# One decode step, attention over a cached K and V: ScalarE sums 80 positions of a middle step, TensorE none

## The chip, the cores and the metric

The kernel runs on one core of a Trainium2 chip. The metric is the time of one execution on the device, in microseconds. Three runs of the kernel before took 665.63, 665.69 and 666.15 us; the median is 665.69.

## The reference

A layer of a decoder for two sequences (B = 2) that each add one token. The attention has 32 heads of 128, each with its own cached K and V of 8192 positions; behind it comes a gated feed-forward part with a width of 1376.

```python
def _A_ref(x, k_cache, v_cache, wq, wo):
    q = transpose((x @ wq).reshape(B, Sq, Hq, Dh), 0, 2, 1, 3)      # Sq = 1, Hq = 32, Dh = 128
    scores = einsum("bhqd,bhkd->bhqk", q, k_cache) * (Dh ** -0.5)   # 8192 positions
    p = softmax(scores)
    o = einsum("bhqk,bhkd->bhqd", p, v_cache)
    return transpose(o, 0, 2, 1, 3).reshape(B, Sq, Hq * Dh) @ wo
def _B_ref(x, W_gate, W_up, W_down):
    gate = x @ W_gate
    h = gate * (gate > 0) * (x @ W_up)
    return h @ W_down
h = x + _A_ref(layernorm(x), k_cache, v_cache, wq, wo)
out = h + _B_ref(layernorm(h), W_gate, W_up, W_down)
```

K and V together are 268 of the 281 MB that the program reads, all in bfloat16.

## The kernel before

**Steps.** K and V come in steps of four heads of one sequence (NH = 4). There are 16 such groups. Steps 0 to 14 are quads; the last group is cut into two halves of two heads, steps 15 and 16 (p0 and p1 in the code). Q = LASTQ = 14 is the last quad; a "middle step" is one below it. A quad's K is a tile of 128 partitions by 32768 elements: 32 partitions to a head, and on each partition 256 positions of 128 elements. So one column of the scores is one position per partition, and a step has 256 columns.

**Buffers.** Three buffers of this size hold K and V in turn: K of step i is in buffer 2i mod 3, V in buffer 2i+1 mod 3 (with exceptions at the end). K of a step and V of the next share a buffer, and so do V of a step and K of the one after next. V of step i+1 can be loaded only once the scores of step i are done with its K, and K of step i+2 only once the values matmuls of step i are done with its V. All these loads are issued by SP, in program order, through `load_tile` (L156 to 163).

**Scores, three ways.** The columns of a step are divided among three engines.

- TensorE scores the last `npe` columns (`scores_pe`, L315): it transposes them in groups of eight into PSUM, ScalarE copies them back (L339), TensorE multiplies with q, which `place_q` has put into the zero-padded `qz` (L277), ScalarE copies the rows out (L347), TensorE turns them, ScalarE puts them into the score columns `scol` (L356).
- For all other columns (`nv`) VectorE multiplies K with q in place (`products`, L360, rows L364).
- Of these, ScalarE sums the first `na` columns, one ACTIVATE with an accumulator to a column (`act_sums`, L366, rows L372), and VectorE the rest, by halving four times (L384) and one reduction (L386) (`scores`, L376).

In a middle step `npe` is 24 and `na` 24; step 0 has `npe` 32; steps 14, 15 and 16 have `npe` 16; steps 15 and 16 have `na` 16.

**Softmax and values.** VectorE takes each partition's maximum (`pm`, L390). TensorE spreads it (`largest`, L397), VectorE reduces it to the negative maximum of each head (`nm`, L402), ScalarE takes four exponentials (L407), and TensorE multiplies 64 times with V (`values`, L420). ScalarE copies the result to `pv` (L425).

**Finished heads.** After steps 3, 7, 11 and 14 a group of heads is finished. `close` (L305) sums the denominators (`z_ps`), takes the reciprocal (`rz`, L299) and normalises (L303). It is called in the step after the group's last. In step 12, `spread` (L455) and `lay_rows` (L466, L467) also lay the first 16 heads out as rows for the projection with wo.

**Order.** The schedule is written by hand; each engine works in program order. In a middle step i of the kernel before: scores of TensorE for step i, q of step i+1 placed, the large products of step i, the sums of VectorE, V of step i+1 loaded, the spread of the maximum, `nm` and exponentials, the first 24 columns of the products of step i+1, ScalarE's 24 sums of them, `close` and (in step 12) `lay_rows`, the values of step i, and K of step i+2 loaded. In step 13 the first products of step 14 stand in front of `nm` of step 13; in step 14 the first products of p0 stand in front of its `nm`.

**The end.** Behind step 14 come wo in pieces, V of p0 and p1, the feed-forward weights, the two halves, the projection, the second layer norm and the feed-forward part.

Of the kernel before, what the change touches and what calls it, by code (L numbers as in the profile page):

```python
# [13 lines left out]
def _free(t, offset, dims):  # L14

    return bass.AP(tensor=t.tensor, offset=t.offset + offset, ap=[t.ap[0]] + [list(d) for d in dims])
# [7 lines left out]
def kernel(  # L24
# [14 lines left out]
    P = nc.NUM_PARTITIONS  # L39
# [8 lines left out]
    f32 = mybir.dt.float32  # L48
# [4 lines left out]
    LASTQ = B * NQ - 2  # L53
# [3 lines left out]
    VG = 4  # L57


    NPE = 24  # L60
    NPE_AT = {0: 32, LASTQ: 16, LASTQ + 1: 16, LASTQ + 2: 16}
    NACT = 24
    NACT_AT = {LASTQ + 1: 16, LASTQ + 2: 16}
    QZ = 32


# [15 lines left out]
    small = ctx.enter_context(tc.tile_pool(name="small", bufs=1))  # L82
# [43 lines left out]
    class Step:  # L126
        def __init__(self, i):
# [9 lines left out]
            else:  # L137
# [6 lines left out]
                self.pg, self.zc = pgp[:, k], zc[:, self.b, self.g, 2 * k:2 * k + 2]  # L144
            self.npe = NPE_AT.get(i, NPE)
            self.nv = self.nt - self.npe
            self.na = NACT_AT.get(i, NACT)
            self.hp = P // self.nh
# [4 lines left out]
    steps = [Step(i) for i in range(LASTQ + 3)]  # L153
    Q = LASTQ
# [28 lines left out]
    with tc.manual_schedule():  # L183
# [92 lines left out]
        def place_q(s):  # L276
            nc.scalar.activation(out=qz[:, QZ - NH:QZ], in_=qTs[:, s.b, NH * s.g:NH * (s.g + 1)], func=ACT.Copy)  # L277
# [27 lines left out]
        def close(i):  # L305
# [4 lines left out]
        scols = {  # L310
            i: qrep[:, c0:c0 + n].rearrange("p i d -> p (i d)").bitcast(f32)
            for i, c0, n in ((Q, 6, 4), (Q + 1, 10, 2), (Q + 2, 12, 2))
        }

        def scores_pe(s, between=lambda: None):  # L315


            U = s.npe // 4
            nh, nv = s.nh, s.nv
            row_ps = ps.tile([nh * U, 4 * P], f32, tag="row")  # L320

            def times_q(c0):
                for k in range(0, TPC, 4):
                    u = (c0 + k) // 4
                    if s.quad:
                        z = qz[:, QZ - NH - NH * u:QZ - NH - NH * u + NH * U]
                    else:
                        z = qzp[:, s.k, 14 - 2 * u:14 - 2 * u + 2 * U]
                    nc.tensor.matmul(  # L329
                        out=row_ps, lhsT=z, rhs=s.kt[:, (nv + c0 + k) * Dh:(nv + c0 + k + 4) * Dh],  # L330
                        start=(u == 0), stop=(u == U - 1),
                    )

            for c0 in range(0, s.npe, TPC):
                t_ps = ps2.tile([P, TPC, P], bf16, tag="tp")
                for k in range(TPC):
                    t = nv + c0 + k
                    nc.tensor.transpose(t_ps[:, k, :], s.kt[:, t * Dh:(t + 1) * Dh], ident)  # L338
                nc.scalar.activation(  # L339
                    out=s.kt[:, (nv + c0) * Dh:(nv + c0 + TPC) * Dh], in_=t_ps.rearrange("p t s -> p (t s)"), func=ACT.Copy,  # L340
                )
                between()
                if c0:
                    times_q(c0 - TPC)
            times_q(s.npe - TPC)
            rows = s.kt[0:nh * U, nv * Dh:nv * Dh + 8 * P].bitcast(f32)
            nc.scalar.activation(out=rows, in_=row_ps, func=ACT.Copy)  # L347
            between()
            sc_ps = ps.tile([P, 4, U, nh], f32, tag="row", name="sc_ps")
            for t in range(4):  # L350
                nc.tensor.transpose(  # L351
                    sc_ps[:, t].rearrange("p u j -> p (u j)"), rows[:, t * P:(t + 1) * P], ident_f[0:nh * U, 0:nh * U],
                )
            for j in range(nh):
                r = s.rows(j)
                nc.scalar.activation(  # L356
                    out=scols[s.i][r, nv:s.nt].rearrange("p (u t) -> p t u", t=4), in_=sc_ps[r, :, :, j], func=ACT.Copy,
                )

        def products(s, t0=0, t1=None):  # L360

            n = (s.nv if t1 is None else t1) - t0
            kv = _free(s.kt, t0 * Dh, [[Dh, n], [1, Dh]])
            nc.vector.tensor_tensor(out=kv, in0=kv, in1=_free(s.qr, 0, [[0, n], [1, Dh]]), op=ALU.mult)  # L364

        def act_sums(s, t0=0, t1=None):  # L366

            if t0 == 0 and s.i < Q:
                scols[s.i] = small.tile([P, s.nt], f32, tag="scol", name="scol")
            for t in range(t0, s.na if t1 is None else t1):  # L370
                kv = s.kt[:, t * Dh:(t + 1) * Dh]
                nc.scalar.activation(out=kv, in_=kv, func=ACT.Copy, accum_out=scols[s.i][:, t:t + 1])  # L372
# [3 lines left out]
        def scores(s):  # L376

            scol = scols[s.i]
            width = Dh
            while width > 8:  # L380
                half = width // 2
                lo = _free(s.kt, s.na * Dh, [[Dh, s.nv - s.na], [1, half]])
                hi = _free(s.kt, s.na * Dh + half, [[Dh, s.nv - s.na], [1, half]])
                nc.vector.tensor_tensor(out=lo, in0=lo, in1=hi, op=ALU.add)  # L384
                width = half
            nc.vector.tensor_reduce(  # L386
                out=scol[:, s.na:s.nv], in_=_free(s.kt, s.na * Dh, [[Dh, s.nv - s.na], [1, 8]]), axis=AXIS.X, op=ALU.add,
            )
            pms[s.i] = small.tile([P, 1], f32, tag="pm", name="pm", bufs=2)
            nc.vector.tensor_reduce(out=pms[s.i], in_=scol, axis=AXIS.X, op=ALU.max)  # L390
# [59 lines left out]
        def spread(k, b):  # L450

            h0, n, _ = SETS[k]
            nq = Dh // n
            sp = qrep[:, B * k + b, :]
            nc.vector.tensor_tensor(  # L455
                out=_free(sp, 0, [[nq, n], [1, nq]]), in0=_free(ocol, h0 * B + b, [[B, n], [0, nq]]),
                in1=_free(quot[n], 0, [[0, n], [1, nq]]), op=ALU.mult,
            )
            return sp

        def lay_rows(k, sps):

            r = SROWS[k]
            or_ps = ps.tile([P, B, r], f32, tag="mx")
            for b in range(B):
                nc.tensor.matmul(out=or_ps[:, b, :], lhsT=sps[b], rhs=rest[r], start=True, stop=True)  # L466
            nc.vector.tensor_copy(orow[k], or_ps.rearrange("p b c -> p c b"))  # L467
# [14 lines left out]
                    start=False, stop=(h == Hq - 1), skip_group_check=True,  # L482
                )

        place_q(steps[0])
        for i in range(Q):
            s = steps[i]
            if i == 0:
                products(s, 0, s.na)
                act_sums(s)  # L490
            scores_pe(s)
            place_q(steps[i + 1])
            products(s, s.na)
            scores(s)
            if i == Q - 2:
                load_tile(A_k_cache, steps[Q], steps[Q].kt)
            else:
                load_tile(A_v_cache, steps[i + 1], steps[i + 1].vt)
            if i == Q - 1:
                scores_pe(steps[Q])  # L500
            largest(s)
            if i == Q - 1:
                products(steps[Q], 0, steps[Q].nv // 4)
            exponentials(s)
            if i < Q - 1:
                products(steps[i + 1], 0, steps[i + 1].na)
            act_sums(steps[i + 1])
            if i - 1 in groups:
                close(i - 1)
            if i == 12:  # L510
                lay_rows(0, [spread(0, b) for b in range(B)])
            half = s.nt // VG // 2
            values(s, 0, half)
            if i == Q - 1:
                load_tile(A_k_cache, steps[Q + 1], steps[Q + 1].kt)
            values(s, half, 2 * half)
            if i in groups:
                diagonals(i)
            if i + 2 < Q:
                load_tile(A_k_cache, steps[i + 2], steps[i + 2].kt)  # L520
            elif i == Q - 2:
                load_tile(A_v_cache, steps[Q - 1], steps[Q - 1].vt)
            else:
                load_tile(A_k_cache, steps[Q + 2], steps[Q + 2].kt)


        s, p0, p1 = steps[Q:]
        products(s, s.nv // 4)
        scores(s)
        load_tile(A_v_cache, p0, p0.vt)  # L530
        largest(s)
        products(p0, 0, p0.nv // 4)
        exponentials(s)
        for k, (h0, n, at) in enumerate(SETS):
            nc.sync.dma_start(
# [8 lines left out]
            out=wo[:, (HM + 2) * D:Hq * D].rearrange("p (h n) -> p h n", n=D),  # L544
            in_=_dram(A_wo, (HM + 2) * Dh * D, [[D, P], [Dh * D, 2], [1, D]]),
        )
        products(p0, p0.nv // 4)

        done = [0]
        parts = [0, 6, 8, 10]  # L550

        def values_then_sums():
            some_values()
# [6 lines left out]
                done[0] += 8  # L560

        scores_pe(p0, values_then_sums)
        act_sums(p0, 10)
        some_values()
        load_tile(A_v_cache, p1, p1.vt, pieces=4)
        scores(p0)
# [90 lines left out]
        parts = [(range(0, UP), "of", ps), (range(UP, FC), "tp", ps2)]  # L657
# [53 lines left out]
```

## Time and profile before

| | |
|---|---|
| median of three runs | 665.69 us |
| the profiled execution's own time | 665.04 us |
| its span, first to last instruction | 663.2 us |
| TensorE, matmuls | 359.2 us busy, 54% of the span |
| VectorE | 524.0 us, 79% |
| ScalarE | 243.6 us, 37% |
| GpSimd | 5.1 us, 1% |
| DMA | 281.45 MB, mean 424 GB/s |
| granted TensorE clock, mean | 0.748 |

How to read it: the span is a little shorter than the execution's time. Busy shares are means over the span; a share of DMA engines of 1.00 in a stretch means that all 16 engines moved data all through it, and a stretch can show a little over 1 since a packet's share is not always counted where it falls. PE is TensorE's matmuls, PEld its weight loads, DVE VectorE, ACT ScalarE, SPq the queue of SP that issues the loads. "<-" behind an idle time names what ended it. In the trace of before, `products` is L364, `act_sums` L372, `scores` L384 to L390; in the kernel after, some of these lines move up by one.

### The profile page before, as it was taken

To read this page: it belongs to the slowest core of one execution; us is meant where nothing else is said; L and a number is where in the kernel's file an instruction comes from. 1 tells how busy PE (TensorE), PEld (TensorE's weight loads), DVE (VectorE), ACT (ScalarE), POOL (GpSimd) and SP (SyncE) were. 2 spreads that over 40 slices of the span, in tenths; PEclk is the share of its full clock that TensorE was granted. 3 is DMA by queue.
4 is the path that set the end of the run, shared out by engine and by line. 5 is a ranking of instruction groups with operands and counts; after the bars stand their busy time and mean duration, and the time that the engine had idled before them with its cause. 6 is when DMAs were issued, how large, how long until landed. Compare 5 with 4: busy or idle time off the path is not lost.

```text
span 663.2 us, 5777 instructions
## 1 busy us (share of the span) xinstructions
PE 359.2 (54%) x2103; PEld 164.0 (25%) x2103; DVE 524.0 (79%) x210; ACT 243.6 (37%) x1083; POOL 5.1 (1%) x25
## 2 busy tenths in 40 slices
PE   3530925729184561918358291754819248281996
PEld 1220311304032220403114140321304124130455
DVE  1398696969969596996969699596978959997981
ACT  1171433515153351515335151532614253431650
POOL 2000000000000000000000000000000000000000
PEclk9865775959678695967859596685959659595885
DMA  9999999999999999999999999999999998999997
GB/s 380 443 440 443 443 432 395 443 443 432 435 440 431 415 444 443 419 440 439 435 428 431 443 424 431 431 436 435 435 440 435 423 440 360 423 404 435 422 390 275
DMA packets 8568, 281.45 MB, mean 424 GB/s; under 512 B 858, under 2 KB 2012, under 8 KB 3420
## 3 DMA queue, kind: packets, MB, share of 16 engines
q1 hardware_dynamic: 8536, 281.09, 98.6%
q8 instruction: 16, 0.26, 0.1%
q14 instruction: 12, 0.10, 0.0%
q10 hardware_dynamic: 4, 0.00, 0.0%
HBM read 281.09 MB, written 0.00 MB: 424 GB/s over the span
## 4 chain that ended last, share of the span: by engine, by line
DMA 40%; DVE 39%; PE 17%; ACT 2%; issue 1%; SPq 0%; DVEq 0%; ACTq 0%
DMA tile<-in_A_k_cache_dram 30%; DVE tile L364 19%; DVE tile L384 17%; PE pv_ps L420 15%; DMA tile<-in_A_wo_dram 5%; DMA tile<-in_B_W_up_dram 2%; ACT pgq L407 2%; DVE scol L386 2%; DMA tile<-in_A_wq_dram 2%; PE q_ps L244 1%; DMA tile<-in_B_W_down_dram 1%; PE mx_ps L397 1%; DVE pm L390 0%; DVE nm L402 0%; DVE qrep L386 0%
## 5 line engine op out<-in xcount | busy, mean ns | idle before, releaser
L364 DVE TENSOR_TENSOR tile<-tile,qrep 128x3072 bf16<-128x3072 bf16 (+4 forms) x30 | 235.7, 7887 | 79.8 <-DMA tile<-in_A_k_cache_dram 79.8
L420 PE MATMUL pv_ps<-tile,pgq 128*16 128x512 bf16 x960 | 242.9, 420 | 43.6 <-ACT pgq L407 37.1
L384 DVE TENSOR_TENSOR tile<-tile 128x13312 bf16<-128x13312 bf16 (+7 forms) x68 | 217.7, 3202 | 2.3
L372 ACT ACTIVATE tile<-tile 128x128 bf16<-128x128 bf16 x392 | 114.8, 294 | 72.6 <-DVE tile L364 72.5
L420 PEld LDWEIGHTS <-pgq 128*16 128x16 bf16 x960 | 91.8, 97 | 188.4 <-issue 48.7
L397 PE MATMUL mx_ps<-nscale,pm 128*128 128x128 f32 x34 | 13.2, 491 | 184.9 <-DVE pm L390 184.9
L407 ACT ACTIVATE pgq<-scol,nm 32x256 bf16<-32x256 f32 x56 | 28.3, 505 | 178.6 <-DVE nm L402 177.6
L372 ACT ACTIVATION_READ_ACCUMULATOR tile<-tile 128x1 f32 x392 | 73.0, 186 | 0.0
L397 PEld LDWEIGHTS mx_ps<-nscale,pm 128*128 128x128 f32 x34 | 8.3, 306 | 187.3 <-DVE pm L390 175.8
L339 ACT ACTIVATE tile<-t_ps 128x1024 bf16<-128x1024 bf16 x49 | 48.5, 1021 | 14.3 <-PE t_ps L338 14.0
L329 PE MATMUL row_ps<-tile,qz 128*24 128x512 bf16 (+2 forms) x90 | 28.4, 398 | 26.4 <-ACT tile L339 26.4
L425 ACT ACTIVATE pv<-pv_ps 16x512 f32<-16x512 f32 (+1 forms) x16 | 9.4, 588 | 69.9 <-PE pv_ps L420 69.9
L338 PE MATMUL t_ps<-ident,tile 128*128 128x128 bf16 x392 | 30.1, 231 | 7.8 <-DMA tile<-in_A_k_cache_dram 7.8
L338 PEld LDWEIGHTS <-tile 128*128 128x128 bf16 x392 | 24.2, 104 | 21.6 <-issue 13.3
L386 DVE TENSOR_REDUCE scol<-tile 128x208 f32<-128x1664 bf16 (+1 forms) x14 | 26.3, 1882 | 1.4
L364 DVE TENSOR_TENSOR tile<-tile,qpair 128x7168 bf16<-128x7168 bf16 (+2 forms) x4 | 15.5, 3884 | 4.1 <-DMA tile<-in_A_k_cache_dram 4.1
L402 DVE TENSOR_REDUCE nm<-mx_ps 128x4 f32<-128x128 f32 (+1 forms) x17 | 4.9, 291 | 14.3 <-PE mx_ps L397 14.3
L329 PEld LDWEIGHTS <-qz 128*24 128x24 bf16 (+2 forms) x90 | 7.1, 92 | 35.8 <-issue 31.0
L347 ACT ACTIVATE tile<-row_ps 24x512 f32<-24x512 f32 (+3 forms) x17 | 10.0, 586 | 13.3 <-PE row_ps L329 13.3
L247 DVE CAST tile<-q_ps 2x512 bf16<-2x512 f32 x8 | 5.4, 679 | 11.8 <-PE q_ps L244 11.8
L244 PE MATMUL q_ps<-tile,xn 128*2 128x512 bf16 x32 | 10.0, 477 | 8.6 <-DMA tile<-in_A_wq_dram 8.6
L356 ACT ACTIVATE scol<-sc_ps 32x24 f32<-32x24 f32 (+1 forms) x56 | 11.5, 205 | 8.2 <-PE sc_ps L351 7.2
(117 smaller groups left out, 129.9 us busy)
## 6 DMA issues: line engine op xcount, KB each, us to landing
tile<-in_A_k_cache_dram SPq DMA_DIRECT2D x2, 4096.0 KB, 24.1
tile<-in_A_wq_dram SPq DMA_DIRECT2D x1, 4096.0 KB, 12.3
tile<-in_A_v_cache_dram SPq DMA_DIRECT2D x1, 4096.0 KB, 23.8
tile<-in_A_v_cache_dram SPq DMA_DIRECT2D x4, 1024.0 KB, 12.5
tile<-in_A_wo_dram SPq DMA_DIRECT2D x1, 2048.0 KB, 28.2
tile<-in_B_W_gate_dram SPq DMA_DIRECT2D x1, 1376.0 KB, 16.0
tile<-in_B_W_up_dram SPq DMA_DIRECT2D x2, 688.0 KB
tile<-in_A_wo_dram SPq DMA_DIRECT2D x1, 1024.0 KB, 30.2
```

The lines of the kernel that those rows point to most:

```text
L244: nc.tensor.matmul(out=q_ps, lhsT=xn[:, c, :], rhs=wq_sb[:, c, n0:n0 + 4 * Dh], start=(c == 0), stop=(c == KC - 1),)
L329: nc.tensor.matmul(out=row_ps, lhsT=z, rhs=s.kt[:, (nv + c0 + k) * Dh:(nv + c0 + k + 4) * Dh], start=(u == 0), stop=(u == U - 1),)
L338: nc.tensor.transpose(t_ps[:, k, :], s.kt[:, t * Dh:(t + 1) * Dh], ident)
L339: nc.scalar.activation(out=s.kt[:, (nv + c0) * Dh:(nv + c0 + TPC) * Dh], in_=t_ps.rearrange("p t s -> p (t s)"), func=ACT.Copy,)
L356: nc.scalar.activation(out=scols[s.i][r, nv:s.nt].rearrange("p (u t) -> p t u", t=4), in_=sc_ps[r, :, :, j], func=ACT.Copy,)
L364: nc.vector.tensor_tensor(out=kv, in0=kv, in1=_free(s.qr, 0, [[0, n], [1, Dh]]), op=ALU.mult)
L372: nc.scalar.activation(out=kv, in_=kv, func=ACT.Copy, accum_out=scols[s.i][:, t:t + 1])
L384: nc.vector.tensor_tensor(out=lo, in0=lo, in1=hi, op=ALU.add)
L386: nc.vector.tensor_reduce(out=scol[:, s.na:s.nv], in_=_free(s.kt, s.na * Dh, [[Dh, s.nv - s.na], [1, 8]]), axis=AXIS.X, op=ALU.add,)
L397: nc.tensor.matmul(out=mx[s.i], lhsT=_free(pms[s.i], 0, [[0, P]]), rhs=nscale, start=True, stop=True)
L407: nc.scalar.activation(out=s.pg[r, :, j, :], in_=scol[r, :].rearrange("p (u t) -> p u t", t=VG), func=ACT.Exp, scale=SCALE, bias=nm[r, j:j ...
L420: nc.tensor.matmul(out=pv_ps[s.i][r, :], lhsT=s.pg[:, u].rearrange("p j t -> p (j t)"), rhs=s.vt[:, u * VG * Dh:(u + 1) * VG * Dh], start= ...
```

## The change

- In steps 0 to 13 TensorE scores no columns any more (`npe` 0): `scores_pe` and `place_q` are called for step 14 and the halves alone.
- In these steps ScalarE sums the first 80 columns instead of 24. VectorE multiplies all 256 columns, instead of 232 (224 in step 0), and sums 176 instead of 208 (200 in step 0).
- In step 14 ScalarE sums 64 columns instead of 24 (VectorE 176 instead of 216), in each half 24 instead of 16 (VectorE 88 instead of 96).
- The products that are made ahead for the next step have 48 columns instead of 24, and ScalarE sums these 48 ahead; the remaining 32 follow once the large products of the step are issued.
- The products ahead and their sums are put behind `close` and `lay_rows` in program order. In steps 13 and 14, `nm` no longer has the first products of the next step in front of it.
- The score columns are allocated by `column` instead of in `act_sums`.

```diff
-    NPE = 24
-    NPE_AT = {0: 32, LASTQ: 16, LASTQ + 1: 16, LASTQ + 2: 16}
-    NACT = 24
-    NACT_AT = {LASTQ + 1: 16, LASTQ + 2: 16}
+    NPE = 0
+    NPE_AT = {LASTQ: 16, LASTQ + 1: 16, LASTQ + 2: 16}
+    NACT = 80
+    NACT_AT = {LASTQ: 64, LASTQ + 1: 24, LASTQ + 2: 24}
+    NEXT = 48
...
-            if t0 == 0 and s.i < Q:
-                scols[s.i] = small.tile([P, s.nt], f32, tag="scol", name="scol")
...
-        place_q(steps[0])
+        def column(s):
+            scols[s.i] = small.tile([P, s.nt], f32, tag="scol", name="scol")
+
+        column(steps[0])
+        products(steps[0], 0, NEXT)
+        act_sums(steps[0], 0, NEXT)
         for i in range(Q):
             s = steps[i]
-            if i == 0:
-                products(s, 0, s.na)
-                act_sums(s)
-            scores_pe(s)
-            place_q(steps[i + 1])
-            products(s, s.na)
+            products(s, NEXT)
+            act_sums(s, NEXT)
             scores(s)
             if i == Q - 2:
                 load_tile(A_k_cache, steps[Q], steps[Q].kt)
             else:
                 load_tile(A_v_cache, steps[i + 1], steps[i + 1].vt)
-            if i == Q - 1:
-                scores_pe(steps[Q])
             largest(s)
-            if i == Q - 1:
-                products(steps[Q], 0, steps[Q].nv // 4)
             exponentials(s)
-            if i < Q - 1:
-                products(steps[i + 1], 0, steps[i + 1].na)
-            act_sums(steps[i + 1])
             if i - 1 in groups:
                 close(i - 1)
             if i == 12:
                 lay_rows(0, [spread(0, b) for b in range(B)])
+            if i + 1 < Q:
+                column(steps[i + 1])
+            products(steps[i + 1], 0, NEXT)
+            act_sums(steps[i + 1], 0, NEXT)
             half = s.nt // VG // 2
             values(s, 0, half)
...
+        place_q(steps[Q])
+        scores_pe(steps[Q])
         s, p0, p1 = steps[Q:]
-        products(s, s.nv // 4)
+        products(s, NEXT)
+        act_sums(s, NEXT)
         scores(s)
         load_tile(A_v_cache, p0, p0.vt)
         largest(s)
-        products(p0, 0, p0.nv // 4)
         exponentials(s)
...
-        products(p0, p0.nv // 4)
+        products(p0, 0, p0.na)
+        products(p0, p0.na)
...
-        parts = [0, 6, 8, 10]
+        parts = [0, 8, 16, 20]
...
-        act_sums(p0, 10)
+        act_sums(p0, 20)
```

## The prediction

> **What bounds the kernel now.** I read the page's slices first, then the busy shares by stretch, then the order of the work inside one middle step, and last the place where the DMA share falls. The slices:
>
> ```profile
> DMA  9999999999999999999999999999999998999997
> GB/s 380 443 440 443 443 432 395 443 443 432 435 440 431 415 444 443 419 440 439 435 428 431 443 424 431 431 436 435 435 440 435 423 440 360 423 404 435 422 390 275
> ```
>
> The DMA engines are busy nearly everywhere, while VectorE (DVE) has 79% of the span and ScalarE (ACT) 37%. The busy shares by stretch say it sharper (columns: stretch, its length, busy time of PE, PEld, DVE, ACT, POOL, then the granted clock, the DMA share and GB/s):
>
> ```profile
> 304.80:382.68 77.88, 43.26 (x212) 19.20 (x211) 63.85 (x18) 29.33 (x132) 0.00 (x0) 0.76 1.00 433
> ...
> 460.58:538.44 77.86, 39.64 (x205) 17.98 (x202) 63.84 (x18) 29.33 (x132) 0.00 (x0) 0.76 1.01 435
> ...
> 550.00:562.00 12.00, 10.02 (x63) 4.54 (x62) 11.97 (x2) 4.10 (x5) 0.00 (x0) 1.00 0.79 317
> 562.00:592.00 30.00, 17.57 (x85) 7.68 (x85) 29.66 (x10) 13.81 (x68) 0.00 (x0) 0.72 0.98 422
> ```
>
> The first two are two middle steps each: share 1.00, so 38.9 us per step is the time to bring in 16.8 MB, and nothing that engines do faster shortens it. One stretch, 550 to 562, has share 0.79: the engines ran dry. The timeline around it shows why (start, duration, engine, line, operation, idle time before it):
>
> ```profile
> 538.44 1.76 DVE L364 TENSOR_TENSOR tile<-tile,qrep 128x3072 bf16<-128x3072 bf16 x1 [5.43 <-DMA tile<-in_A_k_cache_dram]
> 540.12 0.25 DVE L299 RECIPROCAL rz<-z_ps 128x16 f32<-128x16 f32 x1
> ...
> 540.50 0.48 DVE L455 TENSOR_TENSOR qrep<-ocol,quot 128x128 bf16<-128x128 bf16 x2
> 540.84 0.39 PE L466 MATMUL or_ps<-rest,qrep 128*128 128x16 bf16 x2 [7.16 <-DVE qrep L455]
> 541.16 15.45 PE L420 MATMUL pv_ps<-tile,pgq 128*16 128x512 bf16 x64
> ...
> 556.64 0.33 SPq L161 DMA_DIRECT2D tile<-in_A_v_cache_dram  x1
> ```
>
> This is step 12. Its exponentials ended at 535.57, but TensorE first has to lay the finished heads (L466), which waits for VectorE, which stands at the products of step 13 until K of step 13 lands at 538.44. So the values matmuls start at 541.16, end at 556.6, and only then can SP load V of step 13 into their buffer. The transfer ahead (K of step 14, issued at 531.45) had drained by about 554. Everywhere else the next load is issued about 7 us before the one ahead lands, for instance in step 7:
>
> ```profile
> 306.65 0.31 ACT L372 ACTIVATE tile<-tile 128x128 bf16<-128x128 bf16 x1 [5.31 <-DVE tile L364]
> 306.86 0.19 ACT L372 ACTIVATION_READ_ACCUMULATOR tile<-tile 128x1 f32 x1
> 306.96 0.29 ACT L372 ACTIVATE tile<-tile 128x128 bf16<-128x128 bf16 x1
> ...
> 336.36 0.42 DVE L390 TENSOR_REDUCE pm<-scol 128x1 f32<-128x256 f32 x1
> 336.40 0.33 SPq L161 DMA_DIRECT2D tile<-in_A_v_cache_dram  x1
> ...
> 343.40 1.76 DVE L364 TENSOR_TENSOR tile<-tile,qrep 128x3072 bf16<-128x3072 bf16 x1 [5.45 <-DMA tile<-in_A_k_cache_dram]
> ```
>
> V is issued at 336.40, K ahead of it lands at 343.40. Call the landing of a step's K (here 304.80) L: scores end at L+31.6, the next K lands at L+38.6 to 38.9.
>
> **The change, part by part.**
>
> *Middle step, VectorE.* Products grow by 24 positions, sums shrink from 208 to 176. Slopes come from rows of two sizes: products 26624 elements in 14.018 us and 3072 in 1.758, so 0.521 ns each: +1.60 us. The four additions fall from 7.09+3.62+1.89+1.02 = 13.63 to 6.03+3.09+1.62+0.89 = 11.63 by the slope of the first two: -2.00. The reduction (1664 in 1.886, 768 in 0.954) falls by 0.27. Together -0.67: scores end at L+30.9. This is no gain by itself: DMA covers it. If that cover were gone it would be worth 0.67 a step, 9 us in all.
>
> *Middle step, ScalarE.* The rows above start 0.29 us apart though an ACTIVATE lasts 293 ns and its accumulator read 186, so the two overlap. 24 sums went from 306.65 to 313.7, 0.2915 each. After the change: first product block 3.36 us, first sum at L+3.45, 48 sums to L+17.45, then the copy of pv (0.6; its matmuls ended at 357.34, which is L+13.9 of the next step, so no wait), second block of products done at L+17.3, 32 sums to L+27.4. That is 3.5 us ahead of VectorE. TensorE's 24 transposes, its row matmuls and their evictions (317.2 to 324.1 in that step) go; they lay beside the products and additions, so 0.
>
> [...]
>
> *Maximum and finished heads in front of the next products.* In steps 4 and 8 the closing only moves into the 5 us in which VectorE waits for K: 0. In step 12: pm at 530.7, nm (0.29) at 532.0, then z_ps, reciprocal, normalisation, two spreads and two small matmuls, about 2.3 us by their rows, beside the exponentials, which end at 534.9. Values start at 535.1 instead of 541.16 and take 15.5 to 16.9 (both occur in the chain): V of step 13 is issued at 550.6 to 552.0 instead of 556.64, ahead of 554. The gap closes. Its size: by share, 12 x 0.21 = 2.5 us; by bytes, 12 x (1 - 317/433) = 3.2 us. I take 2.6, nearer the share, which counts engine time, while bytes depend on when a packet is counted. Nothing excludes a small rest of the gap; 0 is the other end.
>
> *What is late next.* V of step 13 lands 2.6 earlier: values of step 13 start at 576.4 (579.03 now, on that DMA). Scores of step 13 end at 538.44+30.9 = 569.3 (571.3 now), and its nm no longer stands behind a 4.15 us product block. V of step 14 would drain at about 594; the K halves behind it are issued at 584.8 and 591.7, when half and all of the values are done. Lead 9 us, no new gap. Step 14: 48 sums end at 588.3, then ScalarE waits at the copy of pv until 591.7, places q, evicts for TensorE (563.43 to 568.6 in the trace, 5.2 us) and adds 16 more sums: 602.4; VectorE is done at 601.0. So pm at 602.4 (604.36 now) and nm at 603.7 instead of 610.83, where it stood behind a product waiting for K. SP's order is kept: V of half 15 and the wo loads follow at 602.4, with the K halves still draining until about 613. Half 15: K lands at 606.3, VectorE needs 1.8+6.0+6.1+0.9, pm at 621.4 (624.99 now); ScalarE's 24 sums, in parts of 8, 8 and 8 between evictions, end near 618. Half 16: pm near 637 against 643.36, with its 24 sums from 628 to 635. Compute thus leads by 4 to 6 us where DMA leads by 2.6, so V of half 16, the weights, and the last W_down (landing at 660.01 now) end the program 2.6 earlier.
>
> *Sum.* The profiled execution took 665.04 us (span 663.2 and 1.8 around it), 0.65 below the median of 665.69. 665.04 - 2.6 = 662.4; against the median 663.1.
>
> [...]
>
> **The rivals.**
>
> A. ScalarE becomes the bound (slower). If a sum cost its full 293+186 = 479 ns once 80 follow each other beside VectorE's additions, 80 take 38.3 us and scores end at L+42.4, past the 38.9 of the DMA: a dry spell each step, at least 3.5 us in 13 steps, some 710 us. It decides from (38.9-1.1-4.05)/80 = 0.42 us a sum, taking about 1.1 us from issue to first data. Against it: 0.2915 held over 24 in a row with VectorE's products and TensorE running, and also at 634 to 639 beside VectorE's additions.
>
> B. The gap closes and the end does not follow (within 0.2%). In the last microseconds hm is ready at 657.65 and W_down lands at 660.01. Were the compute at the end not to move at all, y would come near 659.4 instead of 660.36: 1.0 us, 664.7. This decides if ScalarE's longer sums in half 16 (24 for 16, +2.3 us) meet a pm that has not moved; for it, pm of half 15 waited for a sum by 0.4 us; against it, the 4 to 6 us above.
>
> C. The gap does not close: values of step 12 stay late, because TensorE still waits for something of step 13. 665.7. Against it: by program order the spreads no longer have the products in front of them.
>
> **How the numbers follow.** My forecast, a closed gap, has 0.80; B 0.07, C 0.05; A and any other new dry spell 0.08. A change of 0.2%, 1.3 us, is about what a measurement here can tell from none, so B and C count as the same: faster 0.80, same 0.12, slower 0.08. The forecast's own range is 662.2 to 663.9: the gap's 2.5 to 3.2, a rest of it, and runs that spread by 0.5. Taken to B it ends at 665.0; A is left out.
>
> **What would show it.** Right: values of step 12 start near 535 and V of step 13 is issued near 551; the share from 550 to 562 is 1.00; K landings in the middle stay 38.9 apart; VectorE waits for no ScalarE sum before pm in middle steps; W_down lands near 657.4. Wrong: pm in a middle step waiting for L371, sums more than 0.3 us apart, or a stretch below share 0.95 that is new.

## The result: 1.2% slower, and the profile after

The kernel after takes 673.86 us (median of 4 runs, 673.53 to 674.69) beside 665.92 for the kernel before (665.63 to 667.29). The ratio is 1.012, with a 95% interval of 1.010 to 1.0135. The forecast was 663.1. So the change costs 7.9 us where 2.6 were to be gained, and the profiled span grows from 663.2 to 671.9 us.

The slices of the page after:

```profile
DMA  9999999999999999999999999999999999999986
GB/s 375 437 437 437 438 430 437 437 438 434 437 434 434 434 437 433 411 437 422 434 421 431 394 437 433 431 395 433 434 425 431 425 414 437 434 419 429 383 306 233
```

The loads run nearly without a break, as before. In the middle there are small dips (394 and 395 at the lowest), and nothing there looks like a loss of 6 us; the last two slices are emptier than before (306 and 233 for 390 and 275).

Inside a step nearly everything came as it was worked out. Here is step 7 of the kernel after, from the timeline (start, duration, engine, line, operation, idle time before it):

```profile
308.30 17.29 DVE L365 TENSOR_TENSOR tile<-tile,qrep 128x6144 bf16<-128x6144 bf16 x2 [6.75 <-DMA tile<-in_A_k_cache_dram]
311.74 0.31 ACT L371 ACTIVATE tile<-tile 128x128 bf16<-128x128 bf16 x1 [7.67 <-DVE tile L365]
311.96 0.19 ACT L371 ACTIVATION_READ_ACCUMULATOR tile<-tile 128x1 f32 x1
312.05 0.29 ACT L371 ACTIVATE tile<-tile 128x128 bf16<-128x128 bf16 x1
...
335.55 0.30 ACT L371 ACTIVATE tile<-tile 128x128 bf16<-128x128 bf16 x1
335.75 0.19 ACT L371 ACTIVATION_READ_ACCUMULATOR tile<-tile 128x1 f32 x1
337.47 1.62 DVE L385 TENSOR_REDUCE scol<-tile 128x176 f32<-128x1408 bf16 x1
339.15 0.33 SPq L162 DMA_DIRECT2D tile<-in_A_v_cache_dram  x1
339.19 0.42 DVE L389 TENSOR_REDUCE pm<-scol 128x1 f32<-128x256 f32 x1
...
348.35 17.29 DVE L365 TENSOR_TENSOR tile<-tile,qrep 128x6144 bf16<-128x6144 bf16 x2 [7.50 <-DMA tile<-in_A_k_cache_dram]
```

K lands at L = 308.30. The sums are 0.29 us apart, the last of 80 ends at L+27.6, and VectorE's scores end at L+30.9; the forecast had 27.4 and 30.9. SP issues the next V at once. But the next K lands at 348.35, L+40.05, not L+38.9.

The place where the forecast saw its gain is step 12:

```profile
506.41 17.29 DVE L365 TENSOR_TENSOR tile<-tile,qrep 128x6144 bf16<-128x6144 bf16 x2 [6.76 <-DMA tile<-in_A_k_cache_dram]
...
537.30 0.42 DVE L389 TENSOR_REDUCE pm<-scol 128x1 f32<-128x256 f32 x1
...
540.38 0.40 PE L465 MATMUL or_ps<-rest,qrep 128*128 128x16 bf16 x2 [0.76 <-DVE qrep L454]
...
540.88 0.50 ACT L406 ACTIVATE pgq<-scol,nm 32x256 bf16<-32x256 f32 x1
...
541.53 15.40 PE L419 MATMUL pv_ps<-tile,pgq 128*16 128x512 bf16 x64 [0.74 <-ACT pgq L406]
```

The heads are laid out (L465) beside the exponentials, the values matmuls wait for the exponentials alone, and V of step 13 is issued 50.6 us after K of step 12 landed, at 556.96; in the kernel before it was 56.8 us. That step works as forecast too. Only K of step 12 had landed 6.55 us later than before (506.41 against 499.86), and so nothing was gained. The landing in the kernel before:

```profile
499.86 15.69 DVE L364 TENSOR_TENSOR tile<-tile,qrep 128x3072 bf16<-128x3072 bf16 x2 [6.13 <-DMA tile<-in_A_k_cache_dram]
```

The busy shares by stretch show the time that is lost (columns as in the prediction; first two middle steps three times, then the old gap, then the end):

```profile
189.74:269.00 79.26, 36.65 (x146) 15.71 (x145) 62.95 (x20) 53.01 (x338) 0.00 (x0) 0.70 1.00 434
308.30:388.00 79.70, 36.18 (x146) 15.68 (x144) 63.16 (x21) 53.11 (x338) 0.00 (x0) 0.70 0.99 423
427.11:506.41 79.30, 33.96 (x133) 13.30 (x132) 62.51 (x19) 53.13 (x338) 0.00 (x0) 0.69 0.99 423
550.00:562.00 12.00, 6.93 (x33) 2.70 (x30) 12.00 (x1) 12.00 (x84) 0.00 (x0) 0.98 1.01 438
...
630.00:645.00 15.00, 14.76 (x114) 7.12 (x112) 14.76 (x11) 10.73 (x58) 0.00 (x0) 1.00 0.71 278
```

Two steps take 79.3 to 79.7 us where they took 77.9, at a share of DMA engines that still reads 0.99 to 1.00: by the share alone the DMA looks as busy as before. Only the bytes fall, from 433 to 435 GB/s to 423 in two of the three stretches. From 550 to 562 the share is 1.01, so the gap has closed. And 630 to 645 is a new hole, 0.71; in the kernel before this stretch had

```profile
630.00:645.00 15.00, 14.15 (x128) 7.67 (x127) 12.76 (x13) 7.41 (x41) 0.00 (x0) 0.94 1.01 387
```

What differs in the DMA is small. In the list of DMA queues, the kernel before and the kernel after have (packets, MB, share of 16 engines):

```profile
q8 instruction: 16, 0.26, 0.1%
q14 instruction: 12, 0.10, 0.0%
```

```profile
q8 instruction: 12, 0.20, 0.1%
q14 instruction: 25, 0.20, 0.1%
```

The profile counts these packets as `instruction`, so they are taken here for fetches of instructions. A q14 fetch has 8192 bytes, a q8 fetch 16384. One of the 25 packets is no fetch: it has 80 bytes, takes 9 ns and starts 0.06 us into the span, and in the kernel before its like starts 0.06 us ahead of the span. So there are 24 fetches against 12. (The expectations below count 25.) The number of q14 fetches follows ScalarE's count of instructions, which the page of the profile has as x1083 before and x2636 after: 1553 more in 12 more fetches, 129 to a fetch. Each of the 840 added sums is two instructions.

Twelve more fetches of 8 KB are a tenth of a megabyte in 281, and would be forgotten by any mean over 16 engines. The trace's records of single packets show why they count. Around one q14 fetch in the kernel after, the packets that follow each other on one DMA engine are (start ns, duration ns, bytes, queue):

```
198957   309    8192  q14
199263  2762   65536  q1
202021  2418   65536  q1
204436  2418   65536  q1
```

A 64 KB packet of a load takes 2418 ns (3392 of the 3840 in the kernel before). Behind this fetch it takes 2762. The fetch and the slower packet take 0.65 us out of this one engine. And by how the packets follow each other in time, nearly all q14 fetches while the loads run go to the same engine: at least 7 of 12 before, and 15 of the first 16 after (later the records no longer tell this engine apart for sure). By the same chains a load of K or V is 8 packets of 64 KB in a row on each engine, 512 KB. As the others have no more than this one, it can catch up only while they have nothing to move.

Each load ends with a packet of 4 bytes on every engine, 16 before each landing (9 ns each). Their times (us), for K of steps 2, 6 and 12:

```
                    K of step 2            K of step 6            K of step 12
                 median  2nd   last     median  2nd   last     median  2nd   last
before            109.1 110.3  110.4     264.1 265.2  265.2     496.9 498.4  499.4
after             109.0 110.5  110.7     263.8 265.1  268.6     500.0 502.1  506.1
```

After the change one engine is 3.4 us behind the next by K of step 6, and 4.0 at step 12. VectorE starts a step when the last one is done (K of step 12: last at 499.4 and VectorE at 499.86 before, 506.1 and 506.41 after, while the median engine was done at 496.9 and 500.0). The others then wait for loads that are issued only when that step has gone on.

The chain that ended last closes like this (start, duration, what):

```profile
606.74 4.79 ACT tile L371 x32
613.34 34.26 DMA tile<-in_A_wo_dram
647.66 15.87 DMA tile<-in_B_W_up_dram
663.55 5.16 DMA tile<-in_B_W_down_dram
```

The first row is step 14's last sums, behind which SP issues V of half 15 and the wo pieces (611.54; 604.35 before). SP then stood in the issue of a later piece of wo (L538) from 613.34 to 640.68, before from 606.19 to 632.02. By V of step 14 the late engine was 5.4 us behind the next (605.4 and 600.0). The other engines ran out of loads while SP stood there, and the number of engines at work fell from 16 at 635 to 1 at 640. That is the hole from 630 to 645: (1 - 0.71) x 15 = 4.4 us of all engines. What let SP go on is not shown. Here it was shortly after the late engine had done the first piece of wo (about 640); in the kernel before, two engines finished that piece only at 632.4 and 632.6, behind SP's release. W_down lands at 668.71 (660.01 before): 6.55 of the 8.7 us were there at K of step 12, 2.1 came later.

### The profile page after: what moved, and what is told of

It reads as the page before. It is cut to its first block, busy times and chain, and to the rows that moved or that the text cites. A ratio compares the mean times of both kernels' runs of the same rounds, so it can differ in the third digit from the quotient of the medians.

```text
span 671.9 us, 6341 instructions
## 1 busy us (share of the span) xinstructions
PE 304.2 (45%) x1617; PEld 133.9 (20%) x1617; DVE 512.2 (76%) x210; ACT 424.8 (63%) x2636; POOL 5.1 (1%) x25
## 4 chain that ended last, share of the span: by engine, by line
DMA 42%; DVE 33%; PE 20%; ACT 4%; issue 1%; SPq 0%; DVEq 0%; ACTq 0%
DMA tile<-in_A_k_cache_dram 29%; PE pv_ps L419 19%; DVE tile L365 18%; DVE tile L383 12%; DMA tile<-in_A_wo_dram 5%; DMA tile<-in_A_v_cache_dram 4%; ACT pgq L406 2%; DMA tile<-in_B_W_up_dram 2%; DVE scol L385 2%; PE mx_ps L396 1%; DMA tile<-in_B_W_down_dram 1%; ACT tile L371 1%; DVE pm L389 0%; DVE nm L401 0%; ACT tile L340 0%
## 5 line engine op out<-in xcount | busy, mean ns | idle before, releaser
L371 ACT ACTIVATE tile<-tile 128x128 bf16<-128x128 bf16 x1232 | 360.3, 294 | 112.3 <-DVE tile L365 112.1
L365 DVE TENSOR_TENSOR tile<-tile,qrep 128x6144 bf16<-128x6144 bf16 (+2 forms) x30 | 258.3, 8652 | 90.4 <-DMA tile<-in_A_k_cache_dram 90.4
L371 ACT ACTIVATION_READ_ACCUMULATOR tile<-tile 128x1 f32 x1232 | 229.9, 187 | 0.0
L383 DVE TENSOR_TENSOR tile<-tile 128x11264 bf16<-128x11264 bf16 (+3 forms) x68 | 186.7, 2746 | 2.3
L385 DVE TENSOR_REDUCE scol<-tile 128x176 f32<-128x1408 bf16 x14 | 22.7, 1620 | 1.4
L365 DVE TENSOR_TENSOR tile<-tile,qpair 128x7168 bf16<-128x7168 bf16 (+2 forms) x4 | 15.5, 3885 | 2.3 <-DMA tile<-in_A_k_cache_dram 2.3
L431 PE MATMUL o_ps<-pick,pv 128*128 128x16 f32 (+1 forms) x32 | 6.7, 347 | 20.5 <-ACT pv L424 20.5
L431 PEld LDWEIGHTS o_ps<-pick,pv 128*128 128x128 f32 x32 | 6.3, 293 | 21.9 <-ACT pv L424 14.9
L406 ACT ACTIVATION_READ_ACCUMULATOR pgq<-scol,nm 32x1 f32 x56 | 10.3, 184 | 0.0
L340 ACT ACTIVATE tile<-t_ps 128x1024 bf16<-128x1024 bf16 x6 | 6.0, 1023 | 2.8 <-PE t_ps L339 2.6
L419 PE MATMUL pv_ps<-tile,pgp 128*8 128x512 bf16 x32 | 7.1, 379 | 0.0
## 6 DMA issues: line engine op xcount, KB each, us to landing
tile<-in_A_v_cache_dram SPq DMA_DIRECT2D x4, 1024.0 KB, 12.5
tile<-in_A_wo_dram SPq DMA_DIRECT2D x1, 1024.0 KB, 30.9
```

The lines of the kernel that those rows point to most:

```text
L340: nc.scalar.activation(out=s.kt[:, (nv + c0) * Dh:(nv + c0 + TPC) * Dh], in_=t_ps.rearrange("p t s -> p (t s)"), func=ACT.Copy,)
L385: nc.vector.tensor_reduce(out=scol[:, s.na:s.nv], in_=_free(s.kt, s.na * Dh, [[Dh, s.nv - s.na], [1, 8]]), axis=AXIS.X, op=ALU.add,)
L406: nc.scalar.activation(out=s.pg[r, :, j, :], in_=scol[r, :].rearrange("p (u t) -> p u t", t=VG), func=ACT.Exp, scale=SCALE, bias=nm[r, j:j ...
L419: nc.tensor.matmul(out=pv_ps[s.i][r, :], lhsT=s.pg[:, u].rearrange("p j t -> p (j t)"), rhs=s.vt[:, u * VG * Dh:(u + 1) * VG * Dh], start= ...
L431: nc.tensor.matmul(out=o_ps[i][:, 0:n], lhsT=pv[:, t * Dh:(t + 1) * Dh], rhs=pick[:, t].rearrange("p k j -> p (k j)")[:, h0 % (4 * NH):h0 ...
```

## The experiments

Theory F: each ScalarE fetch takes about 0.6 us out of the one engine that the loads wait for; the 12 more make the 7.9 us. Theory O: the new order of heads, maximum and products costs the time. Theory T: ScalarE's sums read and write so much of SBUF beside the loads that these get slower. All runs are compared with runs of the kernel before in the same series: 666.26 us for the first four, 666.06 for the others.

**1. The new order alone.** The kernel before with the shares left as they are:

```diff
-            if i == Q - 1:
-                products(steps[Q], 0, steps[Q].nv // 4)
             exponentials(s)
-            if i < Q - 1:
-                products(steps[i + 1], 0, steps[i + 1].na)
-            act_sums(steps[i + 1])
             if i - 1 in groups:
                 close(i - 1)
             if i == 12:
                 lay_rows(0, [spread(0, b) for b in range(B)])
+            products(steps[i + 1], 0, steps[i + 1].na if i < Q - 1 else steps[Q].nv // 4)
+            act_sums(steps[i + 1])
...
+        exponentials(s)
         products(p0, 0, p0.nv // 4)
-        exponentials(s)
```

> Only the order is changed: in the kernel before, the closing of finished heads and the laying of rows stand in front of the next step's products, and each nm stands in front of the next step's products in steps 13 and 14; the shares of the engines stay (24 positions by TensorE, 24 by ScalarE). Theory F: in the changed kernel each fetch of 8 KB of ScalarE instructions takes some 0.6 to 0.75 us from the one DMA engine that fetches them, all other loads wait for that engine, and the new order does what was forecast. Then this kernel gains the closed gap, 2.6 us against before: 663.3 us, with no stretch of low DMA share between 550 and 562 and 12 fetches on the instruction queue of ScalarE (q14) as before. Rival O (the new order itself delays the loads): slower than before, 668 to 674. Rival T (ScalarE's traffic on the SBUF slows the loads): about 663, as F.

Measured: 665.49 us (665.03 to 666.46), ratio 0.999 [0.998, 0.9999]. Fetches of q14: 12, as before. The stretches:

```profile
550.00:562.00 12.00, 7.83 (x61) 3.86 (x59) 11.93 (x3) 7.06 (x12) 0.00 (x0) 0.90 1.00 431
562.00:592.00 30.00, 15.76 (x60) 6.40 (x60) 28.80 (x9) 10.85 (x61) 0.00 (x0) 0.64 1.00 431
```

O falls: the order costs nothing. But F's own forecast of 663.3 falls with it, as it still had the gap at 2.6 us. The gap is closed (share 1.00 for 0.79), and 0.8 us are gained, just clear of noise. The packets show where the rest went. In the gap of the kernel before, 15 engines idled for 1.3 to 4.1 us, 2.9 in the mean; the engine with the fetches ended K of step 14 only at 557.97 and idled for 0.0. The gap was time in which it caught up. So V of step 13, though issued 5.2 us earlier in this run (551.47 for 556.64), lands only 0.7 earlier (577.5 for 578.2). V of step 14 lands 1.9 earlier (596.8 for 598.7), but the one engine is still 1.9 us behind the next there (0.9 before), and at the wo pieces the lead is lost: SP's held issue ends at 631.83 for 632.02, from 630 to 636 this run has a share of 0.84 where the kernel before has 1.00, and in these two single executions W_down lands at 660.18 for 660.01.

**2. Idle ScalarE instructions, 64 a step.** The kernel before, with

```diff
+    IDLE = 64
...
             scores_pe(s)
             place_q(steps[i + 1])
+            for _ in range(IDLE):
+                nc.scalar.activation(out=warm, in_=eps_col, func=ACT.Copy)
             products(s, s.na)
```

> The kernel before with 64 more ScalarE instructions in each middle step, each on one element that nobody needs, put where ScalarE is idle (after the scores of TensorE). 14 x 64 = 896 instructions, at 128 to a fetch 7 more fetches. Theory F: slower by 7 x 0.6 to 0.75 us = 4.2 to 5.3 us, 670 to 671, with 19 fetches on q14, and the landings of K in the middle 0.3 to 0.4 us further apart per step. Rival T: they move nearly no data, so 665.9, within 0.2%. Rival O: 665.9.

Measured: 686.08 us (684.01 to 687.45), ratio 1.030 [1.027, 1.033], 19 fetches. This is far more than F's 670 to 671, and the trace shows a second cause, one of my making:

```profile
334.37 14.96 ACT L495 ACTIVATE warm<-eps_col 128x1 f32<-128x1 f32 x64
341.50 0.33 SPq L162 DMA_DIRECT2D tile<-in_A_v_cache_dram  x1
342.77 0.29 DVE L403 TENSOR_REDUCE nm<-mx_ps 128x4 f32<-128x128 f32 x1 [0.88 <-PE mx_ps L398]
349.24 0.49 ACT L408 ACTIVATE pgq<-scol,nm 32x256 bf16<-32x256 f32 x1
```

An idle ACTIVATE takes 0.23 us, and 64 of them stand in front of the exponentials until 349.24, 6.2 us after nm. The values, and with them the load of K, come that much later. The run separates nothing, and was made again with half as many.

**3. No accumulator.** The kernel after; ScalarE copies the 80 columns of a middle step without summing them, so each sum is one instruction instead of two, and the scores of those positions are zeros (that part of the computation is left out):

```diff
-                nc.scalar.activation(out=kv, in_=kv, func=ACT.Copy, accum_out=scols[s.i][:, t:t + 1])
+                if s.i < Q:
+                    nc.scalar.activation(out=kv, in_=kv, func=ACT.Copy)
+                else:
+                    nc.scalar.activation(out=kv, in_=kv, func=ACT.Copy, accum_out=scols[s.i][:, t:t + 1])
...
+            nc.gpsimd.memset(scols[s.i][:, 0:s.na], 0.0)
```

> The changed kernel, in which ScalarE copies the 80 positions of each middle step as before but without an accumulator, so with one instruction to a position instead of two; the scores of these positions are zeros, set by GpSimd, so that part of the computation is left out. ScalarE's reads and writes of K stay the same. 1120 instructions fewer, 8 to 9 fetches fewer. Theory F: 673.9 - 8.75 x 0.6 to 0.75 = 667.3 to 668.6, with 16 to 17 fetches on q14. Rival T: the traffic is the same, so 673.9, or more if the copies follow each other faster. Rival O: 673.9.

Measured: 666.98 us (666.63 to 667.59), ratio 1.0009 [1.000, 1.002], 15 fetches, K of step 12 at 501.19. The same columns are read and written, and with 9 fetches fewer 6.9 of the 7.9 us are gone.

**4. Sums over one element.** The kernel after; each sum of a middle step reads and writes one element instead of 128 (the rest of its sum is left out), with as many instructions as before:

```diff
             for t in range(t0, s.na if t1 is None else t1):
                 kv = s.kt[:, t * Dh:(t + 1) * Dh]
+                if s.i < Q:
+                    kv = kv[:, 0:1]
```

> The changed kernel, in which each of ScalarE's sums in a middle step reads and writes one element instead of 128, with its accumulator as before: the same number of instructions, 1/128 of the data; the scores of these positions are wrong, the sums being left out. Theory F: the fetches are the same 25, so about 673.9, at most 1 us off. Rival T: the traffic is gone, so the loads run as forecast, 663. Rival O: 673.9.

Measured: 673.59 us (673.21 to 674.02), ratio 1.011 [1.0095, 1.013], 24 fetches, K of step 12 at 506.90. ScalarE's busy time falls from 424.8 to 306.4 us, less than run 3's 322.2, and the time stays. The fetches are as many as in the kernel after. T falls, and so does any theory by which ScalarE is too busy: the count of instructions decides, not what they do.

**5. Idle ScalarE instructions, 32 a step.** As run 2, with IDLE = 32.

> The kernel before with 32 idle ScalarE instructions (a copy of one element per partition) behind TensorE's scores in each of the 14 quads before the last: 448 more. They take some 6 of the 14 us that ScalarE idles in a step, so that the exponentials should not come later. Theory F (each ScalarE instruction fetch, 8 KB, takes 0.5 to 0.65 us out of the one DMA engine that nearly all of them go through, and the loads land with that engine): 448 instructions are 3.5 more fetches, 1.8 to 2.3 us, so 667.9 to 668.4 beside a kernel before at 666.1, and K landings of middle steps 39.05 to 39.1 apart where they were 38.9. The rival of the 64 idle instructions (they delay the exponentials and that alone cost the 20 us): no change, 666.1.

Measured: 668.61 us (667.94 to 668.81), ratio 1.0035 [1.002, 1.005], 15 fetches; that is 0.2 us above F's range. The exponentials follow nm at once (339.27, 339.59), and yet K of step 12 lands 2.4 us later than before:

```profile
111.16 15.69 DVE L365 TENSOR_TENSOR tile<-tile,qrep 128x3072 bf16<-128x3072 bf16 x2 [5.71 <-DMA tile<-in_A_k_cache_dram]
...
502.27 15.70 DVE L365 TENSOR_TENSOR tile<-tile,qrep 128x3072 bf16<-128x3072 bf16 x2 [6.12 <-DMA tile<-in_A_k_cache_dram]
```

That is 39.11 us a step (38.90 before). Here K of step 12 is done on the median engine at 497.5 (496.9 before), on the last at 501.8 (499.4): most engines are nearly as they were, one is late (the next one is done at 499.3). Instructions that do nothing, added to the kernel before, make the loss of the kernel after in small.

**6. Idle GpSimd instructions, 64 a step.** The kernel before, with

```diff
+    pool_t = consts.tile([P, 1], f32)
...
+            nc.gpsimd.tensor_copy(pool_t, pms[s.i])
+            for _ in range(64):
+                nc.gpsimd.memset(pool_t, 0.0)
             largest(s)
```

> The kernel before with 64 idle GpSimd instructions (a memset of one element per partition) behind each quad's maximum, 14 x 65 in all. GpSimd does nothing else there. Theory F in its narrow form (ScalarE's fetches alone sit on one DMA engine) expects a change only as far as GpSimd's fetches do the same: with 8 KB to 128 instructions 7 fetches, between 0 (spread over the engines, as TensorE's are) and 4.2 us (all on the same engine): 666.1 to 670.3. The rival that the number of fetches decides, whoever makes them and wherever they go, expects the 4.2 us.

Measured: 667.21 us (666.18 to 667.56), ratio 1.0014 [1.0005, 1.002]. There are 7 more q14 fetches, 19 in all, for 910 instructions: 130 to a fetch. But the landings do not move:

```profile
110.82 15.69 DVE L365 TENSOR_TENSOR tile<-tile,qrep 128x3072 bf16<-128x3072 bf16 x2 [5.59 <-DMA tile<-in_A_k_cache_dram]
...
499.84 15.69 DVE L365 TENSOR_TENSOR tile<-tile,qrep 128x3072 bf16<-128x3072 bf16 x2 [5.69 <-DMA tile<-in_A_k_cache_dram]
```

By the packets, five of the new fetches (at 70, 226, 304, 460 and 538 us) went to another single engine than ScalarE's ten. That one was then no later than ScalarE's, and the loads waited for no one new. The number of fetches, wherever they go, is not what costs. The 1.15 us that the run lost lie behind step 12's K: in its profile the values matmuls of step 12 took 16.63 us (15.45 before), and with K of step 13 0.4 later V was issued at 558.21 for 556.64. The granted clock from 541 to 549 was 0.63 in that profile and 0.80 in the kernel before's, which fits the longer matmuls; why it was lower is not shown.

**7. The other way round.** The new order, with TensorE scoring 32 columns of every middle step and ScalarE summing none there; steps 14 to 16 as before (against the kernel of run 1; the moved allocation of the score columns is not printed):

```diff
-    NPE = 24
-    NPE_AT = {0: 32, LASTQ: 16, LASTQ + 1: 16, LASTQ + 2: 16}
-    NACT = 24
-    NACT_AT = {LASTQ + 1: 16, LASTQ + 2: 16}
+    NPE = 32
+    NPE_AT = {LASTQ: 16, LASTQ + 1: 16, LASTQ + 2: 16}
+    NACT = 0
+    NACT_AT = {LASTQ: 24, LASTQ + 1: 16, LASTQ + 2: 16}
...
-            products(steps[i + 1], 0, steps[i + 1].na if i < Q - 1 else steps[Q].nv // 4)
-            act_sums(steps[i + 1])
+            if i == Q - 1:
+                products(steps[Q], 0, steps[Q].nv // 4)
+                act_sums(steps[Q])
```

> The new order of finished heads and products, but the other way round in the shares: TensorE scores 32 columns in every quad before the last and ScalarE sums none there; VectorE sums 224. Step 14 and the halves as in the kernel before. VectorE: 224 products (-0.5 us against 232), 224 sums (+1.1), so scores end at L+32.2, still 6 us ahead of the next landing. ScalarE issues 48 instructions less in each of 14 steps, 672 less, 5 fetches. Theory F: 665.5 (the new order alone) less 5 x 0.5 to 0.65, so 662.2 to 663.0, and K landings 38.7 apart. If ScalarE's fetches were not what paces the loads: 665.5.

Measured: 663.23 us (662.13 to 665.25), ratio 0.996 [0.995, 0.997]. It is faster than both kernels. Its queues and two landings:

```profile
q8 instruction: 17, 0.28, 0.2%
q14 instruction: 7, 0.06, 0.0%
```

```profile
111.08 15.09 DVE L364 TENSOR_TENSOR tile<-tile,qrep 128x28672 bf16<-128x28672 bf16 x1 [5.21 <-DMA tile<-in_A_k_cache_dram]
...
498.81 15.09 DVE L364 TENSOR_TENSOR tile<-tile,qrep 128x28672 bf16<-128x28672 bf16 x1 [4.91 <-DMA tile<-in_A_k_cache_dram]
```

Five fetches fewer than run 1, and 2.1 us less by the two ratios (0.9959 and 0.999 of 666): 0.4 us a fetch, a little under F's 0.5 to 0.65. A step takes 38.77 us. Sixteen packets of 2418 ns, a step's share of one engine, take 38.69, so next to nothing is left to gain in the middle. VectorE is the busiest that it was in any of these kernels but run 8's (532.9 us), and it did not matter.

**8. 48 sums instead of 80.** The kernel after with NACT = 48; VectorE sums 208.

> The kernel after with 48 sums on ScalarE in a middle step instead of 80, all of them ahead; VectorE sums 208. 32 x 2 x 14 = 896 ScalarE instructions less than after, 7 fetches. VectorE's part grows by 2.3 us a step, to L+33.2, still covered. Theory F: 673.9 less 7 x 0.5 to 0.65, 669.3 to 670.4. If the loss came with TensorE scoring nothing, or with any other part that stays: 673.9.

Measured: 669.26 us (668.20 to 669.84), ratio 1.004 [1.003, 1.0055], 17 fetches. The time is F's, but the run says less than that seems to: K of step 12 is done at 500.2 on the median engine and at 502.6 on the last, both some 3.3 us later than before. So here all engines are late, not one. VectorE's longer sums also moved the issue of K to 13.7 to 15.5 us behind the landing in steps 9 to 12 (11.0 to 12.5 in the kernel after), which may have held the other engines up. How much of the loss is which was not separated.

The runs side by side:

```
run                        order   q14 fetches   median us   K of step 12
7 few ScalarE sums          new         7          663.23       498.81
1 order alone               new        12          665.49       500.02
3 no accumulator            new        15          666.98       501.19
8 48 sums                   new        17          669.26       503.11
4 one element               new        24          673.59       506.90
the kernel after            new        24          673.86       506.41
the kernel before           old        12          665.92       499.86
5 idle ScalarE, 32          old        15          668.61       502.27
6 idle GpSimd, 64           old     12 + 7         667.21       499.84
```

Among the runs in the new order, (673.86 - 663.23) / 17 = 0.63 us for each fetch, beside the 0.65 that one fetch takes out of its engine by the packets. It is not the same all along: 0.4 each from 7 to 12, 0.7 from 12 to 24.

## Why the prediction was wrong

**The bound.** "Share 1.00, so 38.9 us per step is the time to bring in 16.8 MB, and nothing that engines do faster shortens it" holds for faster engines. The step that failed is the other half of it, which the sum took for granted: that nothing which engines do, as long as it is hidden, lengthens it ("K landings in the middle stay 38.9 apart"). The share is a mean over 16 engines. The bound was the latest of them, and 38.9 already held 7 fetches in ten steps: with 3 in run 7 it is 38.77.

**ScalarE, middle step.** All times were right: sums 0.2915 apart, done 3.3 us ahead of VectorE. What was missing is a term of the sum: 840 sums are 1680 instructions, and their fetches came between the packets of the loads, mostly on one DMA engine, at about 0.65 us each. It was put at nothing because ScalarE was done in time. Between run 1 and the kernel after, which have the same order, it measured 8.5 us by the two ratios (0.999 and 1.0117 of 666) for 12 fetches. The whole miss, from the forecast's ratio of 0.996 to 1.012, is 10.4 us; the other 1.9 are the size of the gap below. The term could have been bounded: the line of q14 with 12 packets stood in the profile of before beside x1083, and the packets of one fetch could be read there.

**VectorE, middle step.** -0.67 us a step, right, and worth nothing, as the prediction said.

**The finished heads, step 12.** The mechanism was right: values 35.1 us behind K's landing (35.2 forecast), V 50.6 behind it (50.7 to 52.1), a share of 1.0. The size was wrong: 2.6 us were worked out from the mean share (12 x 0.21) and the bytes, and run 1 measured 0.8. The reading behind it was that the transfer ahead "had drained by about 554". At 553.7 the first engine was done with it; the last, which sets the landings, was done at 557.97, behind V's issue, and had not been idle in the gap at all.

**What is late next, and the end.** Compute was to lead by 4 to 6 us where DMA leads by 2.6, so that the loads set the end. They did: W_down's landing closes the chain. But it landed by the slowest engine, and the lag that had grown in the middle came out as the hole at 636 to 641. That the weights "end the program 2.6 earlier" did not hold with the order alone either: in run 1's profile a lead of 1.9 us at V of step 14 was gone at W_down.

**The rivals.** A (ScalarE the bound, 710 us) fell as argued, by the same 0.29 us a sum. C (the gap stays) fell. B's gain of 1.0 us came near the 0.8 of run 1 by luck: run 1's chain still closes with W_down's landing, not with the compute that B names. None of the three held what happened, and the 0.08 for "any other new dry spell" had no mechanism behind it. Of the signs named ahead, two told. K's landings were 39.5 apart (111.17 to 506.41 in ten steps) instead of 38.9. And there was a new stretch below a share of 0.95, 630 to 645, but it lay at the end: in the middle, where 6.55 us were lost, the share stayed at 0.99 over two steps.

## What to carry to other kernels

Where loads run without a break, look for what is slowest among the 16 DMA engines, not at their mean: a share of 1.00 does not say that nothing can be lost (here 6.55 us by step 12 at 0.99 to 1.00), and a hole in the mean may be the time in which the slowest catches up (550 to 562 in the kernel before, where 15 engines idled for 2.9 us in the mean and the slowest for 0.0). Count instructions as DMA traffic: work that is moved to an idle engine in many small instructions (a sum with an accumulator counts twice) can cost more than it frees even if that engine is in time everywhere (7.9 us here). If an engine off the bound can do the same with few instructions, as TensorE and VectorE in run 7 (663.23 us), take it from the one with many.

## What the runs showed of the hardware

- ScalarE's instructions came in packets of 8192 bytes, one to about 129 counted instructions (1553 more in 12 more fetches), GpSimd's in the same size, one to 130 (910 more in 7 more, run 6); q8's have 16384 bytes and numbered 16 before, 12 after and 17 in run 7, where TensorE's matmuls numbered 2103, 1617 and 2233, so they are taken to be TensorE's.
- By how the packets follow each other, the fetches of ScalarE went mostly to one DMA engine within a run (at least 7 of 12 before, 15 of the first 16 after), five of GpSimd's 7 to another one (run 6), and the ten of q8 between 90 and 550 us of the kernel before to at least eight different ones. While K and V load, a q8 fetch costs its engine more than one of q14, 0.88 to 0.97 us and a load packet of 2885 to 2967 ns behind it, 1.4 us in all; but in run 7, with 17 of them and 7 of q14, the last engine was only 0.1 to 0.7 us behind the next at K of steps 2 to 13.
- A q14 fetch takes 309 ns (of the 24 after, two late ones 378 and 384), and the 64 KB packet behind it 2660 to 2950 instead of 2418.
- An ACTIVATE of one element per partition, back to back with others, takes 0.23 us (64 in 14.96, run 2), hardly less than one of 128 elements with its accumulator (0.29, the kernel after).
